# Reading a slot's table entry once, loading the third weight before the fourth slot's rows, and walking the second list backwards in an attention and mixture-of-experts kernel

## The chip, the cores and the metric

One Trainium2 chip, one core. The metric is the device time of one execution in microseconds. The kernel before has three timed runs, 2231.22 to 2242.39 us, median 2234.69 us. A profile of one further execution was taken; its times are in microseconds from the start of its span.

## What is computed

A squared-ReLU attention over 8 batches of 2496 rows, gated by `u`, whose 19968 output rows each go to one of 8 experts, a two-layer network 256 - 1024 - 256:

```python
scores = np.matmul(z, z.transpose(0, 2, 1)) / S
out = np.matmul(np.maximum(scores, 0.0) ** 2, v)
x = (u * out).reshape(B * S, D)
logits = xn @ en.T / tau             # both rows normalized
expert_idx = np.argmax(logits, axis=1)
for e in range(E):
    mask = expert_idx == e
    h = np.maximum(x[mask] @ w1[e], 0.0)
    out[mask] = gate_w[mask, None] * (h @ w2[e])
```

## The kernel before

**Attention stage.** For each batch and each group of 512 columns, TensorE (PE) makes scores and products with `v`. In the background each expert's two weights are split into high and low half-precision parts and written to DRAM as `wsd`. `route` finds the expert of each finished row and `scatter` (L458, on POOL) writes the row into its expert's region of the DRAM tensor `xs`.

**Expert stage.** The sorted rows are worked off in *slots*, numbered k from 0. A first list (A) holds KA = 61 slots of 256 rows and is fixed after seven of the eight batches; a second list (B) holds up to KB = 41 slots of 128 rows for what is left, of which the last NSKIP = 4 stand under an `If` and run only when there are more than 37 tiles. So slots 0 to 60 are list A, and slots 61 to 97 list B. A table in SBUF (`tab`) holds for each slot the place of its rows (row 0), the number of its expert (row 1) and a condition (row 2): whether its expert differs from that of the slot four before.

For each slot:

- `slot_x(k)` reads the place (L800), fetches the rows by a transposing DMA (L807, tile `xt` for slots 0 to 2, `xr` after) and their small columns, gate and row number (L808, `me`, later `mer`);
- `slot_w(k, 0)` and `slot_w(k, 1)` read the number (L813) and, from slot 4 on, the condition (L818), and load the first or the second weight of the expert, 1 MB each, into buffer k % 4 (L816 plain, L819 under the condition; the tiles are called `wa`, `wb` or `w`);
- `slot_up(k)` multiplies the rows by the first weight (L836 to L838), ScalarE and VectorE make the two halves of the ReLU (L840, L841);
- `slot_down(k)` multiplies by the second weight (L860 to L862), VectorE scales (L866), and POOL scatters the rows to the output (L867).

There are NWB = 4 buffers of each weight. Since slot k uses buffer k % 4, the lists are not walked in the order of the experts: `in_turn` cuts the sorted list into four quarters and gives position a to quarter a % 4, so that each buffer sees its quarter's experts in order and a load can mostly be left out by the condition.

**Order on the SP queue.** All of these loads, and the reads of the table ahead of them, are on the SP engine, whose order in this stage is the order of the code (`manual_schedule`). `slot_first` (called half a group before the attention ends) issues the rows of slots 0 to 2, both weights of slot 0 and the first of slot 1. After the attention's pools are closed, `slot_w(1, 1)` follows and then the loop that the change touches. In `work` each turn k issues the rows of slot k + 6 (XAHEAD), the first weight of slot k + 4 and the second weight of slot k + 3. The `mr` pool has eight buffers, so the small tile of slot k + 6 (L808) waits until the output scatter of slot k - 2 has read the old one. TensorE's order is up(0), up(1), down(0), up(2), down(1) and so on.

The table's order comes from numbers that the host passes in: `in_turn` and `last_phase` in `layout`.

Of the kernel before, what the change touches and what calls it, by code (L numbers as in the profile page):

```python
# [27 lines left out]
NWB = 4  # L28
# [3 lines left out]
def ceil_div(a, b):  # L32
    return -(-a // b)


def slot_counts(B, S, E):


    ka = max(0, ceil_div((B - 1) * S - E * (TA - 1), TA))
    return ka, (B * S + E * (TB - 1)) // TB - ka * (TA // TB)  # L40
# [3 lines left out]
def relu2_attention_then_moe(ctx, tc, zT, uT, v, emb, tau, w1, w2, ident, tri, iota_e, out):  # L44
    nc = tc.nc
    B, DQ, S = zT.shape
    D = uT.shape[1]
    E, _, F = w1.shape
# [157 lines left out]
    first = {}  # L206
# [580 lines left out]
    mst = {}  # L787
# [6 lines left out]
    def slot_of(k):  # L794
        return (tables["A"], k, TA) if k < KA else (tables["B"], k - KA, TB)

    def slot_x(k):

        tab, i, T = slot_of(k)
        off = nc.sync.value_load(tab[0:1, 0, i:i + 1], min_val=0, max_val=E * CAP + TB - T)  # L800
        if k < XFIRST:
            xt = mx.tile([P, 4, T], F16, name="xt16", tag="xt16")
            me = mx.tile([P, T // P, ROW - D], F32, name="me", tag="me")
        else:
            xt = mst["mr"].tile([P, 4, T], F16, name="xr16", tag="xr16")
            me = mst["mr"].tile([P, T // P, ROW - D], F32, name="mer", tag="mer")
        nc.sync.dma_start_transpose(xt, xs[bass.ds(off, T), :].bitcast(F16)[:, 0:2 * D])  # L807
        nc.sync.dma_start(me, xs[bass.ds(off, T), D:ROW].rearrange("(j p) w -> p j w", p=P))  # L808
        mst["x", k] = xt, me

    def slot_w(k, i):
        tab, c, _ = slot_of(k)
        e = nc.sync.value_load(tab[0:1, 1, c:c + 1], min_val=0, max_val=E - 1)  # L813
        src = wsd[bass.ds(e, 1), :, (0, WR1)[i]:(WR1, WR1 + WR2)[i]].rearrange("e p w -> (e p) w")
        if k < NWB:
            nc.sync.dma_start(mst["w"][i][k], src)  # L816
        else:
            new = nc.sync.value_load(tab[0:1, 2, c:c + 1], min_val=0, max_val=1)  # L818
            nc.sync.dma_start(mst["w"][i][k % NWB], src, cond=new, cond_hint=False)  # L819

    def slot_up(k):
# [50 lines left out]
    def slot_first():  # L872

        ctx.enter_context(tc.manual_schedule(engines={mybir.EngineType.SP}))
        mst["w"] = ([wp.tile([P, WR1], F16, name="wa0", tag="wr1"), wp.tile([P, WR1], F16, name="wa1", tag="wo")],
                    [wp.tile([P, WR2], F16, name="wb0", tag="wr2")])
        slot_x(0)
        slot_w(0, 0)
        slot_w(0, 1)
        slot_w(1, 0)  # L880
        for k in range(1, XFIRST):
            slot_x(k)
# [39 lines left out]
    for i, (b, g, s) in enumerate(steps):  # L922
# [18 lines left out]
        if b + 1 < B:  # L941
            if (g == NG - 2 and s >= NST - early) or (NG > 1 and g == NG - 1) or NG == 1:
                q = s - (NST - early) if g == NG - 2 else s + early
# [44 lines left out]
    slot_pools()  # L988
    slot_w(1, 1)
    for k in range(2, NWB):  # L990
        slot_x(k + 1)
        slot_w(k, 0)
        slot_w(k, 1)
    for k in range(NWB + 1, XAHEAD):
        slot_x(k)

# [33 lines left out]
def layout(u, v, z, moe_expert_emb, moe_tau, moe_w1, moe_w2):  # L1030
    import numpy as np
    B, S, D = u.shape
    E = moe_expert_emb.shape[0]
    N = B * S
    p = np.arange(P, dtype=np.float32)[:, None]
    rem = S % 512 or 512
    nj = ceil_div(rem, P)

    def in_turn(k):

        a = np.arange(k)
        first = np.cumsum([0] + [ceil_div(k - q, NWB) for q in range(NWB - 1)])
        return (first[a % NWB] + a // NWB).astype(np.float32)

    def last_phase(k):

        m = max(0, k - NSKIP)
        return np.concatenate([in_turn(m), np.arange(m, k, dtype=np.float32)])

    ka, kb = slot_counts(B, S, E)  # L1050

    valid = np.ones((P, 4), np.float32)
    if rem % P:
        valid[rem % P:, 3] = 0.0
    iota = np.concatenate([
        np.tile(E - np.arange(E, dtype=np.float32), (P, 4)),
        p + P * np.arange(4, dtype=np.float32),
        valid,
        np.tile(np.arange(E, dtype=np.float32) * (N + TB), (P, 1)),
        np.tile(np.concatenate([in_turn(ka), last_phase(kb)]), (P, 1)),  # L1060
    ], axis=1).astype(np.float32)
    return {
        "zT": np.ascontiguousarray(z.transpose(0, 2, 1)),
        "uT": np.ascontiguousarray(u.transpose(0, 2, 1)),
        "v": np.ascontiguousarray(v),
        "emb": np.ascontiguousarray(moe_expert_emb),
        "tau": np.ascontiguousarray(moe_tau).reshape(1, 1),
        "w1": np.ascontiguousarray(moe_w1),
        "w2": np.ascontiguousarray(moe_w2),
        "ident": np.eye(P, dtype=np.float32),  # L1070
        "tri": np.triu(np.ones((P, P), np.float32), 1),
        "iota_e": iota,
    }
# [16 lines left out]
```

## Time and profile before

| | us |
|---|---|
| median of three runs | 2234.69 |
| lowest, highest | 2231.22, 2242.39 |
| the profiled execution's own time | 2237.35 |
| its span | 2235.5 |
| first matmul of the expert stage (slot 0) | 1346.1 |
| first matmul of list B (slot 61) | 1989.8 |
| last matmul | 2220.1 |
| TensorE busy | 2156.4 (96%) |
| mean granted TensorE clock | 0.987 of full speed |

SP's instructions and the DMAs that they issue are listed in order of time with the start, the duration on the queue, the line and the tiles; `x2` means two neighbours merged into one row. Register instructions of SP stand in a view by line. In TensorE's rows `ph` is the result of `slot_up`; each slot has its own number there, two in list B, four in list A. The bracket at a row's end gives the idle time ahead of it and what ended it.

### The profile page before, as it was taken

Reading aid. Unit: us, or ns where it says so; the run is one execution under the profiler, and the core shown is the slowest. Engines: PE = TensorE matmul, PEld = TensorE weight load, DVE = VectorE, ACT = ScalarE, POOL = GpSimd, SP = SyncE. Lnnn points to the kernel's source line nnn. Section 1 sums busy time; section 2 is a strip of 40 time slices with the busy share of each in tenths; the row PEclk is TensorE's granted clock in tenths of the full one; section 3 lists DMA queues with packets and bytes.
Section 4 is the critical chain, followed back from the end, with each engine's and each line's share of the span. In section 5 each row is a group of like instructions: output and inputs, shape, how many; then the busy total and the mean of one; then the engine's idle time right before and its main releaser. Section 6 shows DMA issues by size and latency. Waiting matters only on the chain. (4 is left out here: it accounts for less than half of the span.)

```text
span 2235.5 us, 43505 instructions
## 1 busy us (share of the span) xinstructions
PE 2156.4 (96%) x15114; PEld 1419.9 (64%) x15114; DVE 1414.7 (63%) x4293; ACT 1090.1 (49%) x2193; POOL 348.0 (16%) x428
## 2 busy tenths in 40 slices
PE   6999999999999999999999999999999999998986
PEld 2444545444445444545454457888888888898886
DVE  8788889788698788888788655333333333333322
ACT  7577667667567577666676632222222222221111
POOL 0011111111111111111111111211111111111111
PEclk9999999999999999999999999999999999999998
DMA  8858666766847758677665536432233422155343
GB/s 205 186 122 202 153 176 152 185 149 146 219 107 197 172 138 199 148 188 149 146 144 111 101 99 192 118 75 56 70 86 97 100 53 56 44 181 128 83 113 103
DMA packets 523569, 299.00 MB, mean 134 GB/s; under 512 B 443973, under 2 KB 486478, under 8 KB 515920
## 3 DMA queue, kind: packets, MB, share of 16 engines
q1 hardware_dynamic: 508160, 254.93, 49.5%
q0 software_dynamic: 15184, 41.24, 5.4%
q8 instruction: 121, 1.98, 0.4%
q14 instruction: 104, 0.85, 0.1%
HBM read 297.95 MB, written 59.60 MB: 160 GB/s over the span
## 5 line engine op out<-in xcount | busy, mean ns | idle before, releaser
L269 ACT ACTIVATE a<-sc 128x512 f32<-128x512 f32 (+1 forms) x480 | 282.6, 589 | 178.5 <-PE sc L267 141.2
L270 ACT ACTIVATE a<-a 128x512 f32<-128x512 f32 (+1 forms) x480 | 300.0, 625 | 13.2
L308 PEld LDWEIGHTS <-vv 128*128 128x128 f16 x1520 | 148.6, 98 | 178.6 <-DVE vv L252 6.0
L860 PE MATMUL po<-w,hh 128*128 128x256 f16 x944 | 257.3, 273 | 0.6 <-ACT hh L840 0.6
L862 PE MATMUL po<-w,hl 128*128 128x256 f16 x944 | 257.3, 273 | 0.0
L861 PE MATMUL po<-w,hh 128*128 128x256 f16 x944 | 257.3, 273 | 0.0
L307 PEld LDWEIGHTS <-vv 128*128 128x128 f16 x1520 | 149.0, 98 | 168.6 <-issue 11.3
L867 POOL DMA_INDIRECT out_dram<-ot,mer x153 | 148.7, 972 | 663.7 <-DVE ot L866 432.5
L306 PEld LDWEIGHTS <-vv 128*128 128x128 f16 x1520 | 149.0, 98 | 161.0 <-issue 1.7
L458 POOL DMA_INDIRECT xs<-row,dsti x160 | 169.1, 1057 | 477.1 <-DMA xs<-row,dsti 343.6
L306 PE MATMUL acc<-tt,vv 128*128 128x512 f16 (+1 forms) x640 | 236.5, 370 | 3.2 <-DVE xt L336 3.0
L308 PE MATMUL acc<-tt,vv 128*128 128x512 f16 (+1 forms) x640 | 236.3, 369 | 0.0
L307 PE MATMUL acc<-tt,vv 128*128 128x512 f16 (+1 forms) x640 | 236.3, 369 | 0.0
L266 PE MATMUL sc<-z 128*128 128x512 f16 (+1 forms) x480 | 183.0, 381 | 9.0 <-DVE z L190 4.7
L866 DVE TENSOR_SCALAR ot<-po,mer,w 128x256 f32<-128x256 f32 x114 | 58.0, 540 | 206.3 <-PE po L862 202.4
L267 PE MATMUL sc<-z,z 128*128 128x512 f16 (+1 forms) x480 | 183.0, 381 | 0.0
L861 PEld LDWEIGHTS <-hh 128*128 128x128 f16 x1272 | 124.5, 98 | 14.7 <-issue 0.8
L862 PEld LDWEIGHTS <-hl 128*128 128x128 f16 x1272 | 124.5, 98 | 14.4
L860 PEld LDWEIGHTS <-hh 128*128 128x128 f16 x1272 | 124.5, 98 | 14.0
L360 ACT COPY x<-pm 128x256 f32<-128x256 f32 x160 | 58.5, 366 | 143.1 <-PE pm L343 141.0
L836 PEld LDWEIGHTS <-w 128*128 128x128 f16 x768 | 77.5, 101 | 27.9 <-DMA w<-wsd 21.9
L361 DVE COPY lg<-pm 128x8 f32<-128x8 f32 x160 | 25.6, 160 | 103.4 <-ACT x L360 101.8
(4160 smaller groups left out, 5343.7 us busy)
## 6 DMA issues: line engine op xcount, KB each, us to landing
w<-wsd SPq DMA_DIRECT2D x73, 1026.0 KB
wa<-wsd SPq DMA_DIRECT2D x50, 1024.0 KB
w<-wsd SPq DMA_DIRECT2D x48, 1024.0 KB
wb<-wsd SPq DMA_DIRECT2D x25, 1026.0 KB
scan<-in_v_dram SPq DMA_DIRECT2D x56, 312.0 KB
vt<-in_v_dram SPq DMA_DIRECT2D x133, 128.0 KB
ut<-in_uT_dram SPq DMA_DIRECT2D x32, 512.0 KB
wr<-in_w_dram SPq DMA_DIRECT2D x16, 1024.0 KB
```

What stands on the lines that cost most here:

```text
L266: nc.tensor.matmul(sc[:, :n], z1[:, ss], z1[:, t0:t0 + n], start=True, stop=False)
L267: nc.tensor.matmul(sc[:, :n], z1[:, ss], z2[:, t0:t0 + n], start=False, stop=True)
L269: state["at"] = nc.scalar.activation(a[:, :n], sc[:, :n], AF.Relu, scale=2.0 ** -SHIFT).ins
L270: nc.scalar.activation(a[:, :n], a[:, :n], AF.Square)
L306: nc.tensor.matmul(acc[k][:, :n], va, ph[:, :n], start=first, stop=False)
L307: nc.tensor.matmul(acc[k][:, :n], va, pl[:, :n], start=False, stop=False)
L308: nc.tensor.matmul(acc[k][:, :n], vb, ph[:, :n], start=False, stop=last)
L458: nc.gpsimd.indirect_dma_start(xs[:, :], bass.IndirectOffsetOnAxis(ap=loc["dsti"][:m, j:j + 1], axis=0), row[:m, j, :], None)
L860: nc.tensor.matmul(o, hh[:, f, t], wh, start=(f == 0), stop=False)
L861: nc.tensor.matmul(o, hh[:, f, t], wl, start=False, stop=False)
L862: nc.tensor.matmul(o, hl[:, f, t], wh, start=False, stop=(f == NF - 1))
L867: nc.gpsimd.indirect_dma_start(out, bass.IndirectOffsetOnAxis(ap=me.bitcast(U32)[:, j, 1:2], axis=0), ot[:, j, :], None, bounds_check=N - ...
```

## The change

Three edits: `slot_w(k, 0)` keeps the number and the condition in registers and `slot_w(k, 1)` takes them from there; in the loop after the attention both weights of slot k go ahead of the rows of slot k + 1; and list B's first 37 positions walk each quarter from its end to its start.

```diff
     def slot_w(k, i):
         tab, c, _ = slot_of(k)
-        e = nc.sync.value_load(tab[0:1, 1, c:c + 1], min_val=0, max_val=E - 1)
+        if i == 0:
+            e = nc.sync.value_load(tab[0:1, 1, c:c + 1], min_val=0, max_val=E - 1)
+            new = None if k < NWB else nc.sync.value_load(tab[0:1, 2, c:c + 1], min_val=0, max_val=1)
+            mst["e", k] = e, new
+        else:
+            e, new = mst.pop(("e", k))
         src = wsd[bass.ds(e, 1), :, (0, WR1)[i]:(WR1, WR1 + WR2)[i]].rearrange("e p w -> (e p) w")
-        if k < NWB:
+        if new is None:
             nc.sync.dma_start(mst["w"][i][k], src)
         else:
-            new = nc.sync.value_load(tab[0:1, 2, c:c + 1], min_val=0, max_val=1)
             nc.sync.dma_start(mst["w"][i][k % NWB], src, cond=new, cond_hint=False)
...
     for k in range(2, NWB):
-        slot_x(k + 1)
         slot_w(k, 0)
         slot_w(k, 1)
+        slot_x(k + 1)
...
-    def in_turn(k):
+    def in_turn(k, back=False):
 
         a = np.arange(k)
-        first = np.cumsum([0] + [ceil_div(k - q, NWB) for q in range(NWB - 1)])
-        return (first[a % NWB] + a // NWB).astype(np.float32)
+        size = np.array([ceil_div(k - q, NWB) for q in range(NWB)])
+        first = np.cumsum(size) - size
+        at = a // NWB
+        return (first[a % NWB] + (size[a % NWB] - 1 - at if back else at)).astype(np.float32)
 
     def last_phase(k):
 
         m = max(0, k - NSKIP)
-        return np.concatenate([in_turn(m), np.arange(m, k, dtype=np.float32)])
+        return np.concatenate([in_turn(m, back=True), np.arange(m, k, dtype=np.float32)])
```

What this does to the order, first on SP at the start of the expert stage, before (`w_17070` is the second weight of slot 1, `xr_17092` the rows of slot 3, `w_17068` the first weight of slot 2; `Atab` and `Btab` are the tables of the two lists, ISA rows are register arithmetic):

```order
L816 DMA w_17070<-wsd 128x4104
L800 TENSOR_LOAD Atab
L800 ISA x2
L807 ISA
L807 DMA_TRANSPOSE xr_17092<-xs 128x4x256
L808 ISA
L808 DMA mer<-xs 128x2x4
L813 TENSOR_LOAD Atab
L813 ISA x2
L816 ISA
L816 DMA w_17068<-wsd 128x4096
```

and the same place on SP after (`w_17061` is the second weight of slot 1, `w_17059` and `w_17062` those of slot 2, `xr_17085` the rows of slot 3):

```order
L821 DMA w_17061<-wsd 128x4104
L814 TENSOR_LOAD Atab
L814 ISA x2
L821 ISA
L821 DMA w_17059<-wsd 128x4096
L821 ISA
L821 DMA w_17062<-wsd 128x4104
L800 TENSOR_LOAD Atab
L800 ISA x2
L807 ISA
L807 DMA_TRANSPOSE xr_17085<-xs 128x4x256
```

Both weights of slot 2 now stand between slot 1's second weight and slot 3's rows.

On SP in list B, the part of one slot's turn that follows its `mer`, before:

```order
L808 DMA mer<-xs 128x4
L813 TENSOR_LOAD Btab
L813 ISA x2
L818 TENSOR_LOAD Btab
L818 ISA x2
L819 ISA
L819 DMA w_17069<-wsd 128x4096
L813 TENSOR_LOAD Btab
L813 ISA x2
L818 TENSOR_LOAD Btab
L818 ISA x2
L819 ISA
```

and after:

```order
L808 DMA mer<-xs 128x4
L814 TENSOR_LOAD Btab
L814 ISA x2
L815 TENSOR_LOAD Btab
L815 ISA x2
L823 ISA
L823 DMA w_17060<-wsd 128x4096
L823 ISA
L823 DMA w_17062<-wsd 128x4104
```

Of the second weight's turn the two reads and their register rows are gone; its address arithmetic and its DMA stay. On TensorE, VectorE and ScalarE no instruction moves. On POOL, at the start of list A, three scatters of the attention's last rows (L458) come ahead of the fifth output scatter, the first of slot 2:

```order
-L867 DMA out_dram<-ot,me 19968x256 x5
+L871 DMA out_dram<-ot,me 19968x256 x4
+L458 DMA xs<-row,dsti 160896x260 x3
+L871 DMA out_dram<-ot,me 19968x256
 L458 DMA xs<-row,dsti 160896x260
-L867 DMA out_dram<-ot,me 19968x256
-L458 DMA xs<-row,dsti 160896x260 x3
```

The fifth output scatter moves behind three scatters into `xs`, and the sixth behind all four, as before behind one.

## The prediction

> **What bounds the kernel now.** I read busy time by stage first, then TensorE's own waits, then the SP queue in order of time.
>
> ```profile
> core 0: us, PE busy (x) PEld busy (x) DVE busy (x) ACT busy (x) POOL busy (x), PEclk, DMA share, GB/s
> 1361.00:1382.00 21.00, 15.71 (x125) 12.97 (x123) 8.86 (x36) 2.62 (x5) 2.08 (x3) 0.84 0.93 264
> 1382.00:1990.00 608.00, 608.00 (x5578) 544.98 (x5576) 222.64 (x380) 138.50 (x232) 116.67 (x120) 1.00 0.33 83
> 1990.00:2041.00 51.00, 50.31 (x672) 47.34 (x669) 18.76 (x30) 10.75 (x18) 10.68 (x11) 1.00 0.42 111
> 2041.00:2221.00 180.00, 159.69 (x2040) 150.45 (x2040) 54.46 (x85) 33.43 (x56) 28.17 (x29) 0.94 0.46 121
> ```
>
> The expert stage begins near 1346 us. From 1382 to 1990 (the first list, slots 3 to 60) TensorE is busy all the time at clock 1.00: nothing the SP queue does earlier can shorten that. It idles in two places only: 5.3 of 21 us around slot 2, and 20.3 of 180 us in the second list (slots 61 to 97), each time with a lower clock. TensorE's waits there, first those around slot 2, then those of the second list:
>
> ```profile
> PE ph__17470 L836 <- DMA w<-wsd: 5.3, 1, 5.3
> ```
>
> ```profile
> PE ph__29031 L836 <- DMA w<-wsd: 5.0, 1, 5.0
> PE ph__29990 L836 <- DMA wa<-wsd: 4.5, 1, 4.5
> PE ph__31771 L836 <- DMA w<-wsd: 4.5, 1, 4.5
> PE ph__30812 L836 <- DMA w<-wsd: 4.0, 1, 4.0
> PE ph__32385 L836 <- DMA w<-wsd: 1.8, 1, 1.8
> ```
>
> All six are first weights that land late. Why late? The SP queue in the second list shows it (start, duration):
>
> ```profile
> 2013.70 0.35 SPq L808 DMA_DIRECT2D mer<-xs  x1
> 2015.67 1.90 SPq L819 DMA_DIRECT2D w<-wsd  x2
> 2018.32 1.25 SPq L807 DMA_TRANSPOSE xr<-xs  x1
> ...
> 2030.77 1.22 SPq L807 DMA_TRANSPOSE xr<-xs  x1
> 2032.25 0.36 SPq L808 DMA_DIRECT2D mer<-xs  x1
> 2034.14 0.07 SPq L819 DMA_DIRECT2D wa<-wsd  x1
> 2035.75 0.07 SPq L819 DMA_DIRECT2D wb<-wsd  x1
> 2036.54 1.25 SPq L807 DMA_TRANSPOSE xr<-xs  x1
> ...
> 2039.95 1.96 SPq L819 DMA_DIRECT2D w<-wsd  x2
> ...
> 2192.75 1.37 SPq L807 DMA_TRANSPOSE xr<-xs  x1
> ```
>
> ```profile
> L836 PE MATMUL ph__27935<-xr,w x8: 219/219/219, 1997.7 to 1998.9; 128*128 128x128 f16 x8
> ```
>
> ```profile
> L836 PE MATMUL ph__28894<-xr,wa x8: 219/219/219, 2034.8 to 2036.0; 128*128 128x128 f16 x8
> ```
>
> ```profile
> L836 PE MATMUL ph__32385<-xr,w x8: 219/219/229, 2201.7 to 2202.9; 128*128 128x128 f16 x8
> ```
>
> ```profile
> 2045.34 0.29 PE L836 MATMUL ph__29031<-xr,w 128*128 128x128 f16 x1 [5.02 <-DMA w<-wsd]
> ```
>
> The three tiles are the first matmuls of slots 62, 69 and 95. Unhindered, TensorE takes (2034.8 - 1997.7) / 7 = 5.30 us a slot. SP issues x of slot 69 at 2018.32 and of slot 97 at 2192.75: 174.4 / 28 = 6.23 us a slot, and the rows in between follow each other at fixed gaps, so it waits for nobody. SP is the slower one: it falls back until slot 70's first weight, issued at 2039.95, is due at 2040.1 (2034.8 + 5.3). It lands 5.4 us after its issue, at 2045.34. **The second list is bound by SP's instructions**, and only slots whose expert changes show it as a stall. From slot 62 to 95 TensorE needs 33 x 5.30 = 174.9 us and takes 204.0: **29.1 us lost**, 19.8 of it the five waits, 9.3 the lower clock after them (2.3 for each of the four long ones). The Trainium skill, TensorE: Matmul & The Clock Gate, Part 1, says that the array runs at half rate until it has been busy for some 3.4 us, which by estimate is 1.7 us a stall, not 2.3. It also lets an idle time under one such window pass, and the trace agrees: after the 1.8 us wait slot 95's matmuls have their usual 219 ns (229 at most). By the Trainium skill's figure the sum below would be 3 us smaller (five long stalls at 1.7 against 9.3 + 2.2).
>
> **Part 1, number and condition read once.** Per slot SP loses one read of the number (L813) and one of the condition (L818). Around 2030 to 2036.5 the rows of two slot_w calls are, in one slot's turn:
>
> ```profile
> L813 SPq TENSOR_LOAD <-Btab x2: 274/274/275, 2032.7 to 2034.3; - x2
> ```
>
> ```profile
> L819 SPq FUSED_REGOPS  x2: 153/162/171, 2033.8 to 2035.4; - x2
> ```
>
> In the second call the reads begin at 2034.3 and the address arithmetic, which stays, at 2035.4: 1.1 us go. 6.23 - 1.1 = 5.13 us a slot, under TensorE's 5.30. The turn without a transfer falls from 5.77 (2030.77 to 2036.54) to 4.67. In the first list the same 1.1 us are worth nothing, TensorE being at 100%. Nothing else appears on SP: its list has 2,472 rows before and 2,072 after, 400 less, and 200 reads of two rows each are just that. So SP stops falling back: by 0.17 us a slot on average it gains. What is late next is a matter of the head start at the list's beginning, where part 3 comes in. There SP waits for scatters, not for itself:
>
> ```profile
> 1982.10 2.22 SPq L819 DMA_DIRECT2D w<-wsd  x2
> ...
> 1995.97 0.33 SPq L819 DMA_DIRECT2D w<-wsd  x1
> ```
>
> ```profile
> 1984.00 0.97 POOL L867 DMA_INDIRECT out_dram<-ot,mer  x1 [2.21 <-DVE hl L841]
> 1992.75 0.97 POOL L867 DMA_INDIRECT out_dram<-ot,mer  x1 [7.78 <-DVE hl L841]
> ...
> 2004.60 0.97 POOL L867 DMA_INDIRECT out_dram<-ot,mer  x1 [7.69 <-DVE ot L866]
> ```
>
> At the join all four buffers get a new expert, 8 MB. A scatter issued behind two of these transfers holds up the next for 7.7 us instead of 2.2, so a megabyte costs about (7.7 - 2.2) / 2 = 2.8 us, and `mer` of slot 68, whose buffer slot 60's last scatter frees, goes only at 2013.70.
>
> **Part 3, second list backwards.** I counted the experts' rows in the reference's own inputs: first list 7, 9, 8, 8, 8, 8, 8, 5 tiles of experts 0 to 7 (sum 61), second list 4, 4, 4, 5, 4, 3, 3, 10 (sum 37, so the last four slots never run). The first list's buffers 0 to 3 end with experts 1, 3, 5, 7. Slot 61 uses buffer 1, so the second list's quarters (10, 9, 9, 9 tiles) go to buffers 1, 2, 3, 0. Forwards they begin with experts 0, 2, 4, 7, backwards with 2, 4, 7, 7. Only one of four then fits: expert 7 in buffer 3, slot 63. Two of eight transfers go, the first of the pair at 1982.10 and that of 1995.97. Seven changes inside the list stay, but move: forwards slots 70, 71, 77, 83, 90, 93, 95 (five of them are the stalls above), backwards 67, 69, 70, 79, 85, 90, 91. So slot 67 is the new danger: it needs a transfer six slots in, where SP has the least head start. With the join as slow as now, its issue is 2015.67 (slot 66) + 4.67 = 2020.3, it lands 5.4 later at 2025.7, and TensorE wants it at 2018.9 + 5.3 = 2024.2: 1.5 us late. With two transfers fewer SP is there up to 2 x 2.8 = 5.6 us earlier: on time by 4.1 us. I take that, because the two lost transfers stand right ahead of the two slow scatters. Slots 69 and 70 follow with SP 0.17 to 0.63 us a slot faster than TensorE; then the head start only grows. The whole 29.1 us go; I leave 0.5 for residues.
>
> **Part 2, third weight ahead of the fourth slot's rows.** At the stage's start, SP, POOL and TensorE:
>
> ```profile
> 1346.82 0.35 SPq L816 DMA_DIRECT2D w<-wsd  x1
> 1361.02 1.26 SPq L807 DMA_TRANSPOSE xr<-xs  x1
> ...
> 1363.70 1.50 SPq L816 DMA_DIRECT2D w<-wsd  x2
> ```
>
> ```profile
> 1349.28 0.96 POOL L458 DMA_INDIRECT xs<-row,dsti  x1 [11.69 <-DVE hl L841]
> ...
> 1358.28 0.96 POOL L458 DMA_INDIRECT xs<-row,dsti  x1 [1.75 <-DMA xs<-row,dsti]
> ```
>
> ```profile
> 1369.15 0.39 PE L836 MATMUL ph__17470<-xt,w 128*128 128x256 f16 x1 [5.29 <-DMA w<-wsd]
> ```
>
> ```profile
> L836 PE MATMUL ph__17702<-xr,w x4: 272/272/273, 1381.9 to 1382.8; 128*128 128x256 f16 x4
> ```
>
> ```profile
> L836 PE MATMUL ph__18023<-xr,wa x4: 272/272/273, 1392.5 to 1393.5; 128*128 128x256 f16 x4
> ```
>
> Slot 3's rows wait until 1361.02 for the scatter of 1358.28; both weights of slot 2 stand behind them and go at 1363.70, so slot 2 starts 5.3 us late, and takes 1381.9 - 1369.15 = 12.8 us to slot 3 where the next takes 10.6: 2.2 more for the clock. Moved ahead, they go at about 1348, beside nothing that waits, and land ten microseconds before 1363.9: 5.3 + 2.2 = 7.5 us. Moved past them on SP: slot 3's rows, and behind these slot 3's weights. The cost: the scatter of 1349.28 then has up to 2 MB more in front, 2 x 2.8 = 5.6 us at most (below nothing is excluded, a transfer more speeds up no scatter). Then slot 3's rows go at 1361.02 to 1366.6 and its weight 2.7 us later, lands at 1369.1 to 1374.7; slot 3 wants it at 1363.9 + 10.6 = 1374.5. So 0 to 0.2 late; I take 0. On POOL three scatters of the last rows pass slot 2's outputs; slot 2's small tiles are not reused by the mr pool, so nobody waits for that.
>
> **Sum.** 7.5 + 29.1 - 0.5 = 36.1 us. The profiled execution took 2237.35 us, so it would take 2201.3. That execution is 2.7 above the median of the runs, 2234.69; against the median I forecast **2199**, 1.6% less.
>
> **Rivals.**
> - *The start is given back.* Slot 3's weight lands later than that and TensorE stalls at slot 3 instead of slot 2, at most for the same 7.5 us. For it: scatters wait for weights, as at the join. Against: the estimate above ends within 0.2 us. The Trainium skill, DMA: Bandwidth & Descriptors, Queues, rings and completion order, speaks for it: an increment lands only after every earlier write of that DMA engine, across its queues; the 7.7 us rows agree. Time 2199 + 7 = 2206.
> - *SP stays the bound.* If what goes is 0.55 us a slot (one read), 6.23 - 0.55 = 5.68 is still 0.38 over TensorE: 11 us by slot 95, less the head start of 4, and two clock spells of 2.3: 2199 + 11 = 2210. Against: the rows give both reads.
> - *Slot 67 is late.* The join doesn't get faster, 1.5 us and a clock spell, again at 69: 2199 + 5 = 2204.
> - *Landing, not issue.* The late weights come from the transfers, not from SP; then only the start is gained: 2234.7 - 7.5 = 2227. Against: the issues are late, 5.4 us after them the data is there each time.
> - *The clock.* With no gaps left TensorE is granted less in the second list. Its 37 slots are 37 x 5.30 = 196 us; all 36 us are eaten at a clock of 196 / 232 = 0.84, and at 0.80 it is slower: 2234.7 - 36 + 49 = 2248. Against: clock 1.00 over 1990 to 2041, in the same work without a gap.
>
> **Chances.** Forecast 0.68, start given back 0.13, SP stays 0.08, slot 67 0.06, landing 0.03, clock 0.02. The range: at the low end everything goes and the run lies as far below its median as the lowest before (3.5): 2199 - 0.5 - 3.5 = 2195, rounded down to 2194. At the high end the two dearer of the likelier rivals, 2210, and 2 of spread: 2212. Half a per cent, 11 us, is about what a measurement of this kernel can tell from no change. Faster by more: the first four cases, 0.95; the same: landing, 0.03; slower: the clock, 0.02.
>
> **What would show it.** Right: no TensorE wait for w or wa after 1346, SP's turns in the second list 4.7 to 5.2 us until it waits at L808 for output scatters, clock 1.00 there, slot 95 some 29 us less behind slot 62, slot 63 without a transfer. Wrong: a wait of TensorE at slot 3, or at slots 67, 69, 70; turns still above 5.3 us; TensorE spending more than 5.3 us a slot without a wait.

## The result, and the profile after

The changed kernel takes 2203.1 us (median of 4 runs, 2200.9 to 2205.9) against 2236.9 us for the kernel before, now with 4 runs: a ratio of 0.985, 95% interval 0.982 to 0.988. The forecast was 2199, 1.6% less, in a range of 2194 to 2212. The profiled execution has a span of 2199.4 us against 2235.5, 36.1 us less.

The starts of slots divide this. They come from the first matmul of each slot's `ph` tile, for slot 0, 61 and 97 of the kernel after in rows like these (duration min/median/max, then the first and the last start):

```profile
L840 PE MATMUL ph__17141<-xt,wa x4: 272/272/273, 1344.1 to 1345.1; 128*128 128x256 f16 x4
```

```profile
L840 PE MATMUL ph__26654<-xr,wa x8: 219/219/219, 1982.7 to 1983.8; 128*128 128x128 f16 x8
```

```profile
L840 PE MATMUL ph__30829<-xr,wa x8: 219/219/219, 2176.1 to 2177.3; 128*128 128x128 f16 x8
```

| us from | before | after | less |
|---|---|---|---|
| span's start to slot 0 (attention) | 1346.1 | 1344.1 | 2.0 |
| slot 0 to slot 3 | 35.8 | 28.5 | 7.3 |
| slot 3 to slot 61 | 607.9 | 610.1 | -2.2 |
| slot 61 to slot 97 | 222.5 | 193.4 | 29.1 |

The first row is not put down to the change: in the thirteen kernels profiled here, whose attention is the same, slot 0 starts anywhere from 1341.7 to 1350.0 us. So the change itself is worth 34.2 us in this execution, 5.1 in the first list and 29.1 in the second.

TensorE's waits from 1320 us to its end in the kernel after:

```profile
PE po L864 <- DMA w<-wsd: 2.0, 1, 2.0
PE ph__17502 L840 <- DVE hl L845: 0.3, 1, 0.3
```

All six waits for weights of before are gone; one new one of 2.0 us has come, beside 0.3 us for VectorE (DVE) in slot 2. Busy time by stage after (the first numbers are the length, then TensorE's busy time; clock, DMA share and GB/s at the end):

```profile
1361.00:1382.00 21.00, 20.75 (x195) 18.46 (x194) 15.19 (x64) 4.79 (x9) 4.35 (x6) 1.00 0.79 192
1382.00:1983.00 601.00, 599.05 (x5491) 536.81 (x5489) 214.71 (x344) 136.16 (x228) 114.89 (x118) 1.00 0.33 82
1983.00:2041.00 58.00, 58.00 (x790) 55.02 (x788) 21.14 (x34) 12.54 (x21) 11.69 (x12) 1.00 0.73 194
2041.00:2176.00 135.00, 135.00 (x1827) 127.95 (x1825) 49.03 (x77) 30.46 (x51) 25.33 (x26) 1.00 0.42 109
```

In the second list TensorE is busy without a gap and the clock is 1.00; of the 2.2 us of idle time left, 1.95 lie between 1382 and 1983. SP in the second list of the kernel after:

```profile
2007.38 0.78 SPq L823 DMA_DIRECT2D w<-wsd  x2
...
2055.49 1.23 SPq L807 DMA_TRANSPOSE xr<-xs  x1
2056.97 0.36 SPq L808 DMA_DIRECT2D mer<-xs  x1
2058.89 0.07 SPq L823 DMA_DIRECT2D wa<-wsd  x1
2059.31 0.07 SPq L823 DMA_DIRECT2D wb<-wsd  x1
2060.12 1.22 SPq L807 DMA_TRANSPOSE xr<-xs  x1
...
2099.55 1.26 SPq L807 DMA_TRANSPOSE xr<-xs  x1
2103.91 0.35 SPq L808 DMA_DIRECT2D mer<-xs  x1
```

The second weight follows the first by 0.42 us instead of 1.61, and the turn takes 4.63 us (2055.49 to 2060.12), where the prediction said 4.67. The small tile behind the rows of 2099.55 goes 4.4 us after them, not 1.5 as at 2055.49: SP has got so far ahead that it is held by output scatters again. The row at 2007.38 holds slot 67's first weight, which slot 67 needs at 2017.1. With the 5.4 us of the kernel before for landing, 4.3 us are left, where the prediction said 4.1; in this kernel the landing itself shows only at slot 6 (below), where it took 6.1.

The new wait stands here, on TensorE and on SP:

```profile
1421.99 0.27 PE L864 MATMUL po<-w,hh 128*128 128x256 f16 x1 [1.95 <-DMA w<-wsd]
```

```profile
1391.54 0.40 SPq L808 DMA_DIRECT2D mer<-xs  x1
1393.50 0.08 SPq L823 DMA_DIRECT2D w<-wsd  x1
1406.58 8.94 SPq L782 DMA_DIRECT2D xs<-pad  x8
1415.92 0.35 SPq L823 DMA_DIRECT2D w<-wsd  x1
```

It is slot 6's second weight (1415.92), a real transfer since buffer 2 goes over to its second expert there. Ahead of it on SP stand the eight pads (`pads`, L782), which fill the ends of the experts' regions; they wait for the last scatters into `xs`, then take 9 us. From its issue to its use 6.1 us pass. In the kernel before the pads and the same weight stood here:

```profile
1413.22 8.45 SPq L782 DMA_DIRECT2D xs<-pad  x8
1423.39 0.18 SPq L819 DMA_DIRECT2D w<-wsd  x1
```

TensorE wanted that weight at about 1429.3 (5.4 us after slot 7's start at 1423.9, as in the kernel after), and did not wait: by this estimate just in time, and only because TensorE was 7.3 us late from slot 2.

### The profile page after: what moved, and what is told of

Its sections match the earlier page's. It is cut to its first block, busy times and chain, and to the rows that moved or that the text cites. A ratio compares the mean times of both kernels' runs of the same rounds, so it can differ in the third digit from the quotient of the medians.

```text
span 2199.4 us, 42931 instructions
## 1 busy us (share of the span) xinstructions
PE 2144.8 (98%) x15114; PEld 1411.1 (64%) x15114; DVE 1415.6 (64%) x4293; ACT 1089.7 (50%) x2193; POOL 351.3 (16%) x428
## 3 DMA queue, kind: packets, MB, share of 16 engines
q8 instruction: 121, 1.98, 0.4%
## 5 line engine op out<-in xcount | busy, mean ns | idle before, releaser
L458 POOL DMA_INDIRECT xs<-row,dsti x160 | 172.0, 1075 | 487.2 <-DMA xs<-row,dsti 336.2
L865 PE MATMUL po<-wb,hh 128*128 128x256 f16 x328 | 89.4, 273 | 0.0
```

Source lines behind the costliest of these rows:

```text
L458: nc.gpsimd.indirect_dma_start(xs[:, :], bass.IndirectOffsetOnAxis(ap=loc["dsti"][:m, j:j + 1], axis=0), row[:m, j, :], None)
L865: nc.tensor.matmul(o, hh[:, f, t], wl, start=False, stop=False)
```

## The experiments

**My theory**: the second list was bound by SP's instructions, and reading once frees it whatever the order of the list; the third weight first gains 7.3 us at slot 2 and loses part of it at slot 6, behind the pads. **Rivals**: the backward order removes the stalls; the transfers land late and SP's instructions don't matter; the wait at slot 6 is the transfer's own.

| kernel | ratio to before, 95% | slot 0 to 61 | slot 61 to 97 |
|---|---|---|---|
| before | 1 | 643.7 | 222.5 |
| changed | 0.985 (0.982 to 0.988) | 638.6 | 193.4 |
| read once alone | 0.988 (0.986 to 0.989) | 642.9 | 193.4 |
| backwards alone | 0.997 (0.996 to 0.998) | 642.7 | 216.1 |
| third weight first alone | 1.000 (0.999 to 1.001) | 643.1 | 221.1 |
| changed, read twice | 0.996 (0.994 to 0.997) | 638.1 | 215.4 |
| changed, second list forwards | 0.986 (0.984 to 0.987) | 640.2 | 193.6 |
| changed, one more read | 0.988 (0.987 to 0.990) | 640.4 | 199.3 |
| changed, four more reads | one run, 2251.8 us | 638.7 | 243.5 |
| changed, pads later | 0.985 (0.983 to 0.986) | 636.6 | 193.4 |
| third weight first and pads later | 0.997 (0.995 to 0.998) | 636.3 | 219.8 |
| pads later alone | 1.000 (0.999 to 1.001) | 643.2 | 221.7 |
| changed, pads later, list forwards | 0.984 (0.982 to 0.987) | 636.6 | 193.4 |

**Read once alone.** The edit of `slot_w`, and nothing else:

```diff
-        e = nc.sync.value_load(tab[0:1, 1, c:c + 1], min_val=0, max_val=E - 1)
+        if i == 0:
+            e = nc.sync.value_load(tab[0:1, 1, c:c + 1], min_val=0, max_val=E - 1)
+            new = None if k < NWB else nc.sync.value_load(tab[0:1, 2, c:c + 1], min_val=0, max_val=1)
+            mst["e", k] = e, new
+        else:
+            e, new = mst.pop(("e", k))
...
-        if k < NWB:
+        if new is None:
...
-            new = nc.sync.value_load(tab[0:1, 2, c:c + 1], min_val=0, max_val=1)
```

> Only the number and the condition are read once; order of the start and both lists as before. Theory (SP's instructions bound the second list): the 29.1 us lost there go, apart from 0 to 3 us at slot 70, whose weight now lands about when it is due; slots 61 to 97 start within 193 to 197 us instead of 222.5. The stall of 5.3 us at slot 2 stays, and no new one at slot 6. About 28 us less than before. Rival (walking backwards, with fewer and earlier transfers, removes the stalls): the second list stays at 222 us, total within 3 us of before.

Measured: 27 us less (2208.0 us). In the whole expert stage TensorE waits once, at slot 2:

```profile
PE ph__17416 L840 <- DMA w<-wsd: 5.3, 1, 5.3
```

The second list takes 193.4 us, as in the changed kernel: with a new expert in all four buffers at the join of the two lists and the forward order, not even slot 70 waits. Most of the result is this one edit.

**Backwards alone.** `in_turn` as in the change, and its call in `last_phase`:

```diff
...
-        return np.concatenate([in_turn(m), np.arange(m, k, dtype=np.float32)])
+        return np.concatenate([in_turn(m, back=True), np.arange(m, k, dtype=np.float32)])
```

> Only the second list is walked backwards; all four reads of a slot and the order of the start as before. Theory: SP still needs 6.2 us a slot against 5.3 of TensorE, so the second list stays bound by SP; it begins some 5 us better because slot 63 has no transfer, and its last transfer is due at slot 91 instead of 95, so about 20 us are lost instead of 29: slots 61 to 97 start within 208 to 218 us. About 9 us less than before. Rival (the order of the list removes the stalls): 193 us, 29 us less than before.

Measured: 6 us less by the ratio (4 to 8 by its interval) where I expected 9; slots 61 to 97 in 216.1 us, near the upper end of what was expected. TensorE's waits from 1980 us on; the five `ph` tiles are slots 79, 85, 90, 69 and 91:

```profile
PE ph__30264 L836 <- DMA w<-wsd: 5.9, 1, 5.9
PE po L860 <- DMA w<-wsd: 4.1, 2, 2.5
PE ph__31086 L836 <- DMA wa<-wsd: 3.3, 1, 3.3
PE ph__31771 L836 <- DMA w<-wsd: 1.9, 1, 1.9
PE ph__28894 L836 <- DMA wa<-wsd: 1.2, 1, 1.2
PE ph__31908 L836 <- DMA w<-wsd: 0.3, 1, 0.3
```

The stalls have moved to the slots where the backward order changes experts; they have not gone. The rival falls.

**Third weight first alone.**

```diff
     for k in range(2, NWB):
-        slot_x(k + 1)
         slot_w(k, 0)
         slot_w(k, 1)
+        slot_x(k + 1)
```

> Only the third weight goes ahead of the fourth slot's rows. Theory: no wait at slot 2, slot 3 starts 7.4 us earlier after slot 0, but slot 6's second weight, which stands behind the eight pads on SP, is now late by 2 to 4 us; so slot 61 starts 4 to 6 us earlier after slot 0 and the second list stays at 222 us: 4 to 6 us less in all. Rival (the start is all given back at slot 3 or later): slot 61 as before, no difference.

Measured: no difference, against the 4 to 6 us that I expected. Slot 3 comes 28.5 us after slot 0, 7.3 less than before, as it should, but slot 61 only 0.6 us earlier. Slot 6:

```profile
1429.79 0.37 PE L860 MATMUL po<-w,hh 128*128 128x256 f16 x1 [5.00 <-DMA w<-wsd]
```

The wait there is 5.0 us and the slower clock behind it 1.7 more (614.6 from slot 3 to slot 61 against 607.9): nearly the whole gain is paid back some 50 us after slot 3's start. My mechanism was right and its size too small. In the other kernels with this edit and the pads in their old place the wait was 1.6 to 2.2 us. The shortest came with the second reads put back (next experiment), where SP has the same instructions in the first list:

```profile
1422.40 0.27 PE L860 MATMUL po<-w,hh 128*128 128x256 f16 x1 [1.59 <-DMA w<-wsd]
```

There the pads started 62.1 us after slot 0, here 65.5. Each is one profiled execution, and what makes SP 3.4 us later here is not shown. So with the pads in their old place the edit is worth 0.6 to 5.6 us up to slot 61, by kernel.

**The changed kernel with the second reads put back.** `slot_w` as before, the other two edits as changed:

```diff
-        if i == 0:
-            e = nc.sync.value_load(tab[0:1, 1, c:c + 1], min_val=0, max_val=E - 1)
...
-        else:
-            e, new = mst.pop(("e", k))
+        e = nc.sync.value_load(tab[0:1, 1, c:c + 1], min_val=0, max_val=E - 1)
...
+            new = nc.sync.value_load(tab[0:1, 2, c:c + 1], min_val=0, max_val=1)
```

> The changed kernel with the second reads put back: backwards and third weight first, but number and condition read twice. Theory: both effects of these two edits add, some 5 us at the start and some 9 us in the second list, and about 20 us of the gain are missing: about 14 us less than before. Rival (the reads cost nothing on the path): as the changed kernel, 34 us less than before.

Measured: 9 us less than before by the ratio, 6 to 12 by its interval; in the profile 5.6 us at the start and 7.1 in the second list. The first was as expected, the second 2 short of it. About 24 us of the changed kernel's gain are missing, so the reads are what it rests on.

**The changed kernel with the second list forwards.**

```diff
-        return np.concatenate([in_turn(m, back=True), np.arange(m, k, dtype=np.float32)])
+        return np.concatenate([in_turn(m), np.arange(m, k, dtype=np.float32)])
```

> The changed kernel with the second list walked forwards. Theory: the reads saved keep SP ahead in either order; slot 63's transfer comes back and costs SP some 5 us of its head start, which is spare by then except at slot 70: 0 to 3 us more than the changed kernel; slots 61 to 97 start within 193 to 197 us. Rival (backwards is needed): 9 us or more over the changed kernel.

Measured: 2203.6 us, the same as changed within the runs' scatter; 193.6 us in the second list, no wait. Once SP is fast enough, the order is worth nothing that can be measured.

**One and four more reads per slot of the second list** (the changed kernel with this in the second call of `slot_w`; `range(4)` for the other):

```diff
             e, new = mst.pop(("e", k))
+            if k >= KA:
+                for _ in range(1):
+                    nc.sync.value_load(tab[0:1, 1, c:c + 1], min_val=0, max_val=E - 1)
```

One more:

> The changed kernel with one more read of the number per slot of the second list, its value unused. A read is 0.55 us on SP. Theory: SP's turn without waits rises from 4.9 to 5.1 us to 5.45 to 5.7, just over TensorE's 5.30; the head start of 10 us less 5.4 for a transfer covers most: 0 to 9 us more than the changed kernel. Rival (landing, not issue): no difference.

Four more:

> The changed kernel with four more reads of the number per slot of the second list, their values unused. Theory: SP's turn is 7.1 to 7.3 us, 1.8 to 2.0 us over TensorE's pace; over 34 slots less a head start of 10 us the second list takes 50 to 65 us more, slots 61 to 97 start within 240 to 262 us, with waits of TensorE at the transfers, and after a while at slots without a transfer too. Rival (landing, not issue): 193 us as in the changed kernel.

Measured: 199.3 and 243.5 us for slots 61 to 97, so 5.9 and 50.1 more, both inside what was expected. From TensorE's waits in the second list of the kernel with four more, the three longest, of slots 85, 79 and 90, and four shorter ones, of slots 84, 76, 78 and 75:

```profile
PE ph__30510 L843 <- DMA wa<-wsd: 7.0, 1, 7.0
PE ph__29580 L843 <- DMA w<-wsd: 6.8, 1, 6.8
PE ph__31285 L843 <- DMA w<-wsd: 5.9, 1, 5.9
...
PE ph__30355 L843 <- DMA wa<-wsd: 2.3, 1, 2.3
...
PE ph__29115 L843 <- DMA wa<-wsd: 1.8, 1, 1.8
PE ph__29425 L843 <- DMA w<-wsd: 1.4, 1, 1.4
PE ph__28960 L843 <- DMA w<-wsd: 1.4, 1, 1.4
```

Slots 75, 76, 78 and 84 have no transfer at all: there TensorE waits for SP merely to get to the skipped load. SP's turn in that kernel:

```profile
2110.69 1.24 SPq L807 DMA_TRANSPOSE xr<-xs  x1
2112.19 0.35 SPq L808 DMA_DIRECT2D mer<-xs  x1
2114.07 0.08 SPq L826 DMA_DIRECT2D wa<-wsd  x1
2117.03 0.08 SPq L826 DMA_DIRECT2D wb<-wsd  x1
2117.84 1.22 SPq L807 DMA_TRANSPOSE xr<-xs  x1
```

From rows to rows it takes 7.15 us against 4.63: 0.63 us a read. No transfer was added, so landing is not the cause; the number of instructions on SP is.

**The pads later.** The changed kernel with the pads at turn 14:

```diff
-    queue += [table_b, pads]
+    queue += [table_b]
...
         for k in range(k0, k1):
+            if k == 14:
+                pads()
             if k + XAHEAD == KA:
```

> The changed kernel with the eight pads put on SP at turn 14 of the first list instead of turn 3. Theory: slot 6's second weight no longer stands behind them, the new wait of 2.0 us at slot 6 goes and nothing takes its place, as no transfer is due between slots 12 and 27: slot 61 starts 2 us earlier after slot 0, total 2 us under the changed kernel. Rival (that wait comes from the transfer's own landing): slot 6's wait stays.

Measured: 2199.0 us median against 2203.6 for the changed kernel with its list forwards, which ran beside it; by the profile slot 61 comes 636.6 us after slot 0, 2.0 less, and TensorE waits for no weight any more. Its one wait in the whole expert stage:

```profile
PE ph__17502 L840 <- DVE hl L845: 0.3, 1, 0.3
```

The ratios' intervals overlap, so the time alone does not show it; the slots do.

**Third weight first with the pads later, and the pads later alone** (both on the kernel before). The first:

```diff
-    queue += [table_b, pads]
+    queue += [table_b]
...
-        slot_x(k + 1)
         slot_w(k, 0)
         slot_w(k, 1)
+        slot_x(k + 1)
...
+            if k == 14:
+                pads()
```

The second has the first and the last piece only.

> The kernel before with the third weight first, and the eight pads on SP at turn 14 of the first list instead of turn 3; reads twice, second list forwards. Theory (what the early weight gains is lost again at slot 6, whose second weight stands behind the pads): no wait in the first list, slot 61 starts 636 to 637 us after slot 0 instead of 643.7, the second list stays at 221 to 223 us; about 7 us less than before. Rival (the loss at slot 6 has another cause): slot 61 at 640 us or more, as with the third weight first alone.

> The kernel before with only the pads moved to turn 14. Theory: with the stall at slot 2 in place slot 6's second weight was just in time anyway, so nothing is gained: slot 61 starts 643 to 644 us after slot 0, no difference from before. Rival (the pads hold up list A by themselves): 2 us or more less.

Measured: 7 us less (ratio 0.997) with 636.3 us to slot 61, and no difference with 643.2. The early weight is worth its full 7 us only with the pads out of the way, and the pads cost nothing as long as the weight is late. On the kernel before each of the two alone is worth nothing. That settles the wait at slot 6.

**The changed kernel with pads later and the list forwards**, the pads as two experiments above and the list as with the second list forwards:

```diff
-    queue += [table_b, pads]
+    queue += [table_b]
...
+            if k == 14:
+                pads()
...
-        return np.concatenate([in_turn(m, back=True), np.arange(m, k, dtype=np.float32)])
+        return np.concatenate([in_turn(m), np.arange(m, k, dtype=np.float32)])
```

> The changed kernel with the pads at turn 14 and the second list walked forwards. Theory: walking backwards is worth nothing once SP is fast enough: slot 61 starts 636 to 637 us after slot 0, slots 61 to 97 start within 193 to 194 us, the same time as with the pads later and the list backwards, about 2199 us. Rival: 2 us or more above that.

Measured: 636.6 and 193.4 us, the same as with the list backwards. The median of 2201.8 us is 2.8 above the 2199.0 there, as the rival has it. But the kernel before, run beside each of the two, took 2.8 longer here as well (2238.1 against 2235.4), and the ratios to it agree: 0.9844 and 0.9845. Two of the three edits and the moved pads do all that there is: in neither list does TensorE wait for a weight.

## Why the prediction was right, and where it was not

- *The second list is bound by SP's instructions, 29.1 us lost, all of it goes.* Right to the tenth: 222.5 to 193.4 us, without the 0.5 left for residues. Shown by reading once alone and by the reads added back. One row was misread: of the 9.3 us put down to the lower clock, 0.65 are a wait of TensorE for ScalarE in slot 71.
- *1.1 us a slot go, the turn falls to 4.67.* Measured 4.63, so 1.14.
- *Backwards, two transfers fewer, slot 67 the new danger and on time by 4.1 us.* On time by some 4 us. But that I counted part 3 as needed for the 29.1 us was wrong: forwards slot 67 has no transfer, and reading once is enough in either order. The danger that the head start guarded against is one that this edit itself brought.
- *Third weight first, 7.5 us; slot 3's weight late by 0 to 0.2.* 7.3 us by slot 3, and no wait at slot 3. The cost came within its bounds: slot 3's rows, issued at 1362.86, go 18.8 us after slot 0's start instead of 14.9, some 4 later of the 5.6 allowed. The step that failed is "moved past them on SP: slot 3's rows, and behind these slot 3's weights", as the whole of what is late next. I followed the queue for one slot. Three slots on, slot 6's second weight behind the pads had no time to spare but what the stall at slot 2 gave it, and took 2.2 us back. The term of 7.5 is 5.1, and "no TensorE wait for w or wa after 1346", a sign of being right, did not come.
- *Sum 36.1.* The span fell by just that, but by luck: 34.2 from the change and 2.0 from an attention stage that happened to be shorter. Of the 4 us between the median of 2203.1 and the forecast of 2199, 2.2 are the median of before, which its fourth run moved from 2234.7 to 2236.9; by the medians the change took 33.8.
- *The rivals.* SP stays the bound, slot 67 late, landing and the clock: none came; the clock is 1.00 with no gap left. "The start is given back" came in part, and not at slot 3 but at slot 6; with the third weight first alone it came in full.

## What to carry to other kernels

When DMAs are issued by one engine, count its instructions per turn against the turn of the engine that it feeds: a queue that never waits and is a sixth too slow (6.23 us against 5.30) shows up only as late transfers, at the turns where there are any, and hides behind them. When a stall is removed, look for the next load on the same queue over as many turns as the stall gave shelter, not only at the one that was passed; an edit that measures nothing alone (third weight first, 1.000) can be worth 7 us once the wait behind it is moved. An edit that comes bundled with two others should be run alone, and the bundle without it, before its share is believed.

## What the runs showed of the hardware

A read of a table entry into SP's registers, with the two register rows behind it, costs 0.57 to 0.63 us of the queue: 1.14 for two by the changed kernel, 2.52 for four by the kernel with four more. A weight load that its condition leaves out still takes 0.07 us there, against 0.35 with the transfer.

A wait of about 2 us may or may not bring the slower clock. With 1.95 us at slot 6 the changed kernel kept 1.00 and lost 2.2 us; with its list forwards the wait was 2.04 us, and in the same stretch of ten microseconds the clock fell and 3.9 us were lost (slot 3 to 61 in 611.8 us against 607.9). First the changed kernel:

```profile
1420.00:1430.00 10.00, 8.05 (x75) 7.17 (x74) 2.41 (x5) 1.20 (x2) 1.95 (x2) 1.00 0.69 126
```

then the one with its list forwards:

```profile
1420.00:1430.00 10.00, 7.96 (x59) 6.36 (x57) 2.04 (x3) 1.20 (x2) 1.95 (x2) 0.83 0.67 166
```

Over all of TensorE's waits for a weight in the expert stages profiled here, and the granted clock in the 3.5 us behind each: none of the 32 waits of up to 1.98 us was followed by a lower clock, 9 of the 15 between 2.04 and 3.75 us were, and all of the 22 of 3.81 us and more. Within the middle range the length does not decide: in the kernel with the pads later alone two waits of 3.75 us were followed by 1.00 (at 2047.47) and 0.65 (at 2129.96).

The Trainium skill, TensorE: Matmul & The Clock Gate, Part 1, says that the activity is judged in windows of some 3.4 us that run freely; that waits of the same length sometimes count and sometimes not is in keeping with this, though no run here shows the windows. The prediction took from the same Part 1 of the Trainium skill that an idle time under one window passes. That holds for its 1.8 us but not in general: waits of 2.04 to 3.33 us brought the slower clock six times, and the measurement decides.
